# ELU parts of a feed-forward layer: the result of the max stays in its PSUM bank

## The chip, the cores and the metric

The kernel runs on one core of one Trainium2 chip. The metric is the device time of one execution in microseconds (us). The core has five engines that work at the same time: TensorE (PE, matrix products, with its weight load PEld), VectorE (DVE), ScalarE (ACT), GpSimd (POOL) and SyncE (SP, which issues most transfers). TensorE writes its products into PSUM, a small memory of eight banks; one bank holds 128 x 512 float32. VectorE and ScalarE read and write PSUM and the large on-chip memory SBUF.

## The reference

Three layers in a row on 2304 tokens (4 batches of 576) of width 512:

```python
x = attention(q, k, v)            # landmark attention, 8 heads of 64
h = x @ w_in                      # 512 -> 2048
g = np.where(h > 0, h, np.exp(np.minimum(h, 0)) - 1)     # ELU
x = g @ w_out                     # 2048 -> 512
out = mixture_of_experts(x)       # top 2 of 8 experts, 512 -> 1024 -> 512
```

The change lies in the second layer, between the two products.

## The kernel before

The feed-forward layer works on six chunks of tokens (512, 256 and four times 384 columns) and on 16 blocks of 128 hidden features. A *part* c.f is block f of chunk c; there are 96 parts. Each value is carried as a float16 high half and a float16 low half, and each product is three float16 products.

The order of all work ahead of the experts is written out by hand: `ORDER` is a list of tokens, and each engine runs its own instructions in the order of that list. Work of the attention (tokens such as `2:nm.1`), the conversion of weights (`I`, `Wa`, `Wb`), the routing (`RA` to `RS`) and the feed-forward layer are mixed in it. One part goes through these tokens:

- `L1.c.f` (line 678): 6 to 12 matmuls put h into a PSUM tile `h`, one bank. The tag "l1" has two banks.
- `X` (ACT): e = exp(h) into an SBUF tile `e`. The tag "el" has two buffers.
- `T` (ACT or DVE line 702, as the last letter says): e becomes min(e, 1) - 1 (or its negative), in place.
- `S` (DVE line 706): e = max(e * scale, h), in place in SBUF. This is the last reader of the bank.
- `H` (ACT): the high half g[:, 0] = float16(e).
- `O` (DVE or POOL line 711): the low half g[:, 1] = e - g[:, 0]. This is the last reader of `e`. [...]
- `L2.c.f.t` (line 718): three matmuls for each 128 tokens add the part's share to the output tile `y`.

All elementwise ACT work is recorded at line 215. A new product `h` gets, of the two banks of its tag, the one whose last use stands earliest in the recorded program, also where that use is recorded after the product's own token. So the banks don't strictly alternate: the tokens `S` are not always in the order of the tokens `L1`. TensorE runs its list in order: while a product waits for its bank, everything behind it on TensorE waits too.

Of the kernel before, what the change touches and what calls it, by code (L numbers as in the profile page):

```python
# [13 lines left out]
ALU = mybir.AluOpType  # L14
# [36 lines left out]
ORDER = """  # L51
# [128 lines left out]
def attn_ffn_moe_kernel(ctx: ExitStack, tc: tile.TileContext, q: bass.AP, k: bass.AP, v: bass.AP,  # L180
# [18 lines left out]
    V, A, G, T = nc.vector, nc.scalar, nc.gpsimd, nc.tensor  # L199
# [14 lines left out]
    def act(o, i, f=AF.Copy, **kw):  # L214
        return A.activation(o, i, f, **kw)  # L215
# [451 lines left out]
            lo += n  # L667

    HX = {}

    def l1(c, f):
        p = ps.tile([128, 512], F32, tag="l1", bufs=2, name=f"h{c}_{f}")[:, :CHUNKS[c][1]]
        fs = slice(128 * (f % 8), 128 * (f % 8) + 128)
        for b, o, n, c0 in segments(c):
            i = 0
            for g in range(2):
                for x, y in ((0, 0), (0, 1), (1, 0)):
                    T.matmul(p[:, c0:c0 + n], GT[b, f // 8][:, g, x, fs], AT[b][:, g, y, o:o + n],  # L678
                             start=(i == 0), stop=(i == 5))
                    i += 1  # L680
        HX[c, f] = [p]

# [11 lines left out]
    def elu(c, f, part, e=V):  # L694
        x = HX[c, f]
        if part == "X":
            x.append(sf.tile([128, 512], F32, tag="el", bufs=2, name=f"e{c}_{f}")[:, :CHUNKS[c][1]])
            act(x[1], x[0], AF.Exp, scale=1.0 / S_H)
        if part == "T":
            x.append(S_H if e is V else -S_H)  # L700
            if e is V:
                V.tensor_scalar(x[1], x[1], 1.0, 1.0, op0=ALU.min, op1=ALU.subtract)
            else:
                act(x[1], x[1], AF.Relu, scale=-1.0, bias=1.0)
        if part == "S":
            V.scalar_tensor_tensor(x[1], x[1], x[2], x[0], op0=ALU.mult, op1=ALU.max)  # L706
        if part == "H":
            HT[c, f] = sf.tile([128, 2, 512], F16, tag="gT", bufs=3, name=f"g{c}_{f}")[:, :, :CHUNKS[c][1]]
            act(HT[c, f][:, 0], x[1])
        if part == "O":  # L710
            e.tensor_tensor(out=HT[c, f][:, 1], in0=x[1], in1=HT[c, f][:, 0], op=ALU.subtract)  # L711
# [555 lines left out]
    for n in "XTSHO":  # L1267
        CMD[n] = lambda c, f, *e, n=n: elu(c, f, n, *e)
# [23 lines left out]
    for e in range(1, NE):  # L1292
# [12 lines left out]
        for i, f0 in enumerate((0, 2)):  # L1305
            more[f0, 1] = [(ew_split, e, j, k) for j in ((6 + i,) if e > 1 else (4 + i, 6 + i)) for k in range(2)]
            x, y = (3, 4) if last else (4, 3)
# [29 lines left out]
    with tc.If(peak > CAP):  # L1337
# [5 lines left out]
        with tc.For_i(0, NE, 1) as e:  # L1343
            V.tensor_scalar(ef, ef, 1.0, None, op0=ALU.add)
            nb = nc.values_load(blocks[0:1, bass.ds(e, 1)], min_val=0, max_val=(NT - CAP + 127) // 128)
            with tc.If(nb > 0):
# [4 lines left out]
                for src, dst, kn, nm, scale in ((w1, w1x, 1, "a", S_W1), (w2, w2x, 2, "b", S_W2)):  # L1351
                    for j in range(4):
# [6 lines left out]
                                               op1=ALU.subtract)  # L1359
                with tc.For_i(0, nb, 1) as i:  # L1360
# [7 lines left out]
                                           op1=ALU.mult)  # L1368
# [56 lines left out]
```

## Time and profile before

| | us |
|---|---|
| median of 3 runs | 784.09 |
| the three runs | 787.2, 784.09, 781.5 |
| the profiled execution | 778.33 |
| its span, first to last instruction | 776.6 |
| PE busy in the span | 752.7 (97%) |
| DVE busy | 619.1 (80%) |
| ACT busy | 427.5 (55%) |
| POOL busy | 279.4 (36%) |

The feed-forward layer lies between 54.6 and 395 us. The profile lists busy time per engine, the waits of each engine with what ended them, and a timeline of instructions. Ends of matmuls are modelled, so a short wait of PE can hide behind the modelled end of the matmul before it.

### The profile page before, as it was taken

How to read it: one execution, taken by the hardware profiler on the slowest of the kernel's cores; microseconds unless marked ns; L12 is line 12 of the kernel's file. 1: busy time of each engine (PE TensorE's matmuls, PEld its weight loads, DVE VectorE, ACT ScalarE, POOL GpSimd, SP SyncE). 2: the span in 40 equal slices, each digit the busy share in tenths (PEclk: the TensorE clock that was granted, in tenths of full speed). 3: DMA queues.
4: the chain of work that ended last, by engine and by line, in shares of the span. 5: the costliest groups of instructions: out<-in, count | busy, mean ns of one | idle time of the engine just before them, and what ended most of it. 6: DMA issues, size and time to landing. Idle time of an engine off the chain costs nothing.

```text
span 776.6 us, 17554 instructions
## 1 busy us (share of the span) xinstructions
PE 752.7 (97%) x6978; PEld 442.5 (57%) x6979; DVE 619.1 (80%) x1352; ACT 427.5 (55%) x820; POOL 279.4 (36%) x302
## 2 busy tenths in 40 slices
PE   8879999999999999999999999999999999999997
PEld 6444444555445446655454874756747576574754
DVE  4999998877886776837547689989999999999851
ACT  2778778646466455546433364656555455664520
POOL 1576566454351222231404252424343332302322
PEclk9999999999999999999999999999999999999999
DMA  9998676786395715523435876673848657382481
GB/s 347 280 299 210 171 243 167 213 180 190 98 255 89 168 42 146 152 87 80 124 42 145 143 248 99 155 186 49 253 73 230 116 135 203 44 241 28 79 268 67
DMA packets 136200, 123.19 MB, mean 159 GB/s; under 512 B 102891, under 2 KB 105963, under 8 KB 136016
## 3 DMA queue, kind: packets, MB, share of 16 engines
q1 hardware_dynamic: 125392, 100.67, 47.9%
q0 software_dynamic: 10720, 21.34, 12.7%
q8 instruction: 56, 0.92, 0.5%
q14 instruction: 32, 0.26, 0.1%
HBM read 70.62 MB, written 39.76 MB: 142 GB/s over the span
## 4 chain that ended last, share of the span: by engine, by line
PE 91%; DVE 5%; DMA 1%; ACT 1%; issue 1%; SPq 0%; POOL 0%; POOLq 0%; DVEq 0%; ACTq 0%
PE y L718 24%; PE ey L1161 21%; PE eb L1066 19%; PE h L678 12%; PE eh L1124 3%; PE ey L1167 3%; PE pg L645 2%; PE ey L1164 2%; DMA q<-in_q_dram 1%; PE pu L483 1%; PE pcv L548 1%; PE l1b L339 1%; PE pe L535 1%; DVE ax L596 0%; DVE woc L259 0%
## 5 line engine op out<-in xcount | busy, mean ns | idle before, releaser
L718 PE MATMUL y<-wout,g 128*128 128x512 f16 x864 | 205.8, 380 | 0.8 <-issue 0.6
L1161 PE MATMUL ey<-w,eh 128*128 128x512 f16 x768 | 167.4, 379 | 0.0
L1187 POOL DMA_INDIRECT acc<-eo,tk x35 | 73.5, 2101 | 204.5 <-ACT eo L215 88.7
L718 PEld LDWEIGHTS <-g 128*128 128x128 f16 x864 | 80.6, 98 | 93.8 <-issue 9.3
L1161 PEld LDWEIGHTS <-eh 128*128 128x128 f16 x768 | 75.0, 98 | 89.0
L678 PE MATMUL h<-AT,G 128*128 128x192 f16 (+3 forms) x768 | 108.0, 286 | 1.4 <-DVE e L706 1.2
L711 POOL TENSOR_TENSOR g<-e,g 128x384 f16<-128x384 f32 (+2 forms) x44 | 43.8, 996 | 135.8 <-ACT g L215 121.1
L678 PEld LDWEIGHTS <-G 128*128 128x128 f16 x768 | 63.7, 98 | 43.6 <-issue 6.2
L215 ACT ACTIVATE eh<-c 128x300 f16<-128x300 f32 x112 | 47.7, 453 | 63.0 <-DVE c L1083 59.0
L215 ACT ACTIVATE g<-e 128x384 f16<-128x384 f32 (+2 forms) x96 | 49.4, 519 | 48.0 <-PE y L718 28.6
L215 ACT ACTIVATE eo<-ey,ws 128x512 f32<-128x512 f32 (+3 forms) x60 | 32.4, 541 | 68.7 <-PE ey L1161 40.2
L215 ACT ACTIVATE e<-h 128x384 f32<-128x384 f32 (+2 forms) x96 | 46.4, 487 | 38.9 <-PE h L678 24.4
L706 DVE SCALAR_TENSOR_TENSOR e<-e,h 128x384 f32<-128x384 f32 (+2 forms) x96 | 52.3, 549 | 15.2 <-ACT e L215 12.6
L903 POOL DMA_INDIRECT xs<-rows,pos x36 | 37.0, 1027 | 58.1 <-DVE mcum L887 26.9
L942 DVE SCALAR_TENSOR_TENSOR w<-ew,w 128x1024 f16<-128x1024 f32 x36 | 44.6, 1261 | 13.2 <-ACT w L215 13.2
L1066 PE MATMUL eb<-tx,wpC 128*128 128x300 f16 x336 | 47.4, 291 | 0.0
L1095 DVE SCALAR_TENSOR_TENSOR eh<-c,eh 128x300 f16<-128x300 f32 x112 | 46.1, 463 | 1.0
L711 DVE TENSOR_TENSOR g<-e,g 128x384 f16<-128x384 f32 (+2 forms) x52 | 29.5, 572 | 13.6 <-ACT g L215 10.8
L1066 PEld LDWEIGHTS <-wpD 128*128 128x128 f16 x336 | 32.7, 97 | 11.0 <-issue 0.9
L1066 PEld LDWEIGHTS <-wpB 128*128 128x128 f16 x336 | 32.8, 98 | 10.0
L1066 PEld LDWEIGHTS <-wpC 128*128 128x128 f16 x336 | 32.7, 97 | 10.2
L1083 DVE TENSOR_TENSOR c<-eb,u 128x300 f32<-128x300 f32 x84 | 36.6, 461 | 1.7 <-PE eb L1066 1.5
(263 smaller groups left out, 1359.9 us busy)
## 6 DMA issues: line engine op xcount, KB each, us to landing
ew<-in_moe_w_dram SPq DMA_DIRECT2D x64, 512.0 KB
wi<-in_moe_w_in_dram SPq DMA_DIRECT2D x16, 512.0 KB
wo<-in_moe_w_out_dram SPq DMA_DIRECT2D x16, 512.0 KB
q<-in_q_dram SPq DMA_DIRECT2D x8, 576.0 KB
k<-in_k_dram SPq DMA_DIRECT2D x8, 576.0 KB
v<-in_v_dram SPq DMA_DIRECT2D x4, 1152.0 KB
out_dram<-acc SPq DMA_DIRECT2D x1, 4608.0 KB
xs<-zrow SPq DMA_DIRECT2D x3, 1300.0 KB
```

Source lines behind the costliest of these rows:

```text
L215: return A.activation(o, i, f, **kw)
L678: T.matmul(p[:, c0:c0 + n], GT[b, f // 8][:, g, x, fs], AT[b][:, g, y, o:o + n], start=(i == 0), stop=(i == 5))
L706: V.scalar_tensor_tensor(x[1], x[1], x[2], x[0], op0=ALU.mult, op1=ALU.max)
L711: e.tensor_tensor(out=HT[c, f][:, 1], in0=x[1], in1=HT[c, f][:, 0], op=ALU.subtract)
L718: T.matmul(YP[c, t], h[:, x, 128 * t:128 * t + 128], WOUT[f][:, y], start=(f == 0 and i == 0), stop=(f == 15 and i == 2))
L903: n = nc.gpsimd.indirect_dma_start(out=xs[:, :], out_offset=bass.IndirectOffsetOnAxis(ap=R["pos"][:, i // 2, i % 2:i % 2 + 1], axis=0), in ...
L942: V.scalar_tensor_tensor(dst[1][:, ks, :], t, scale, dst[0][:, ks, :], op0=ALU.mult, op1=ALU.subtract)
L1066: T.matmul(p, w_op(e, w, s, k, f), x_op(e, x, t, k), start=(i == 0 and k == 0), stop=(i == 2 and k == 1))
L1083: V.tensor_tensor(out=o, in0=EB[n, f], in1=EU[a, f], op=ALU.add)
L1095: V.scalar_tensor_tensor(lo, o, 0.0, hi, op0=ALU.max, op1=ALU.subtract)
L1161: T.matmul(p, EH[e, f][:, x, 128 * j:128 * j + 128], W2T[e][y][:, f, :], start=start, stop=stop)
L1187: nc.gpsimd.indirect_dma_start(out=acc[:, :], out_offset=bass.IndirectOffsetOnAxis(ap=TK[e][:live(j), j:j + 1], axis=0), in_=EO[e, j], in_ ...
```

## The change

For parts whose `O` runs on VectorE and stands in `ORDER` ahead of the second next token `L1`, `S` writes its result into the PSUM bank that holds h instead of into `e`. `H` and `O` then read the bank. 20 of the 96 parts meet the test: 0.1, 1.2, 1.14, 2.4, 2.10, 2.14, 2.15, 3.1, 3.7, 3.8, 3.10, 3.13, 4.0, 4.5, 4.11, 5.2, 5.7, 5.8, 5.14 and 5.15. For these the tile `e` is last used by `S`, and the bank is last used by `O`.

```diff
     HX = {}
+    at = {x: i for i, x in enumerate(ORDER.split())}
+    hs = [x for x in at if x[:3] == "L1."]
+    direct = set()
+    for i, x in enumerate(hs):
+
+        o = at.get(f"O{x[2:]}.V")
+        if o and (i + 2 >= len(hs) or o < at[hs[i + 2]]):
+            direct.add(x[3:])
...
         if part == "S":
-            V.scalar_tensor_tensor(x[1], x[1], x[2], x[0], op0=ALU.mult, op1=ALU.max)
+            o = x[0] if f"{c}.{f}" in direct else x[1]
+            V.scalar_tensor_tensor(o, x[1], x[2], x[0], op0=ALU.mult, op1=ALU.max)
+            x[1] = o
```

No instruction is added, removed or moved on any engine. What moves is which tiles the 60 instructions `S`, `H` and `O` name, which bank 32 of the products get, and who waits for whom. The products behind a changed part in the bank that the built program gives it: h0_2 behind part 0.1, h1_5 behind 1.2, h3_11 behind 3.10, h4_2 behind 4.0. Two products get the other bank than before, since a changed part now keeps its own bank longer: h2_11, which stood behind part 2.10, now stands behind 2.12 (whose `S` is on VectorE just ahead of the `O` of 2.10), and h3_10, which stood behind 3.8, now stands behind 3.9 (whose `S` is recorded after h3_10).

VectorE around part 0.1, the kernel before (`S` is L706, `O` is L711; the name ahead of the arrow is written, those behind it are read, and the brackets name the engines waited for):

```order
L706 SCALAR_TENSOR_TENSOR e0_1_772<-e0_1_772,h0_1_750 128x512 [waits Activation_49]
L292 SCALAR_TENSOR_TENSOR wout0_634<-wo2_389,wout0_634 128x512
L711 TENSOR_TENSOR g0_0_782<-e0_0_769,g0_0_782 128x512 [waits Activation_49]
L259 TENSOR_SCALAR win2_257<-wi21_522 128x512
L260 SCALAR_TENSOR_TENSOR wi21_522<-wi21_522,win2_257 128x512
L711 TENSOR_TENSOR g0_1_797<-e0_1_772,g0_1_797 128x512 [waits Activation_49]
```

The same place with the change (`S` is L715, `O` is L721):

```order
L715 SCALAR_TENSOR_TENSOR h0_1_750<-e0_1_772,h0_1_750 128x512 [waits PE_49,Activation_49]
L292 SCALAR_TENSOR_TENSOR wout0_634<-wo2_389,wout0_634 128x512
L721 TENSOR_TENSOR g0_0_782<-e0_0_769,g0_0_782 128x512 [waits Activation_49]
L259 TENSOR_SCALAR win2_257<-wi21_522 128x512
L260 SCALAR_TENSOR_TENSOR wi21_522<-wi21_522,win2_257 128x512
L721 TENSOR_TENSOR g0_1_797<-h0_1_750,g0_1_797 128x512 [waits Activation_49]
```

The bank of h0_1 is now last read by the last of these rows, before by the first. The next product in that bank, h0_2, waits for VectorE in both kernels: before until the first row is done, now until the last.

TensorE at the product h2_11, the kernel before:

```order
L718 MATMUL y21_2629<-wout2_1147,g2_9_2989 128x512
L483 MATMUL pu23_3090<-R23_3045 32x64 [waits DVE_49]
L483 MATMUL pu23_3090<-R23_3045 32x64 x7
L678 LDWEIGHTS G11_1857
L678 MATMUL h2_11_3101<-AT1_1708,G11_1857 128x384
```

With the change:

```order
L728 MATMUL y21_2629<-wout2_1147,g2_9_2989 128x512
L483 MATMUL pu23_3090<-R23_3045 32x64 [waits DVE_49]
L483 MATMUL pu23_3090<-R23_3045 32x64 x7
L686 LDWEIGHTS G11_1857
L686 MATMUL h2_11_3101<-AT1_1708,G11_1857 128x384 [waits DVE_49]
```

Before, the first matmul of h2_11 had no wait of its own; now it waits for VectorE, for the `S` of part 2.12.

## Rows read from the trace of the kernel before

**Rows 1.** The page: span, then busy us, share of the span, instructions of each engine.
```profile
span 776.6 us, 17554 instructions
PE 752.7 (97%) x6978; PEld 442.5 (57%) x6979; DVE 619.1 (80%) x1352; ACT 427.5 (55%) x820; POOL 279.4 (36%) x302
```

**Rows 2.** Windows, the feed-forward stretch: length, then busy PE, PEld, DVE, ACT, POOL, clock.
```profile
54.60:395.00 340.40, 333.68 (x3133) 173.44 (x3132) 258.19 (x662) 209.76 (x446) 133.61 (x166) 1.00 0.59 152
```

**Rows 3.** The page's chain of work that ended last, by engine.
```profile
PE 91%; DVE 5%; DMA 1%; ACT 1%; issue 1%; SPq 0%; POOL 0%; POOLq 0%; DVEq 0%; ACTq 0%
```

**Rows 4.** Waits of PE in that stretch: us in total, times, longest.
```profile
PE pu L483 <- issue: 2.1, 3, 1.3
PE pa L431 <- ACT lT L215: 1.8, 1, 1.8
PE h L678 <- DVE e L706: 1.2, 2, 1.0
```

**Rows 5.** Timeline of PE: where h0_2, h1_5, h2_11, h3_10, h3_11, h4_2 start.
```profile
60.22 1.02 PE L678 MATMUL h<-AT,G 128*128 128x512 f16 x4
...
138.46 0.83 PE L678 MATMUL h<-AT,G 128*128 128x64 f16 x12
...
211.41 1.15 PE L678 MATMUL h<-AT,G 128*128 128x384 f16 x6
...
268.03 1.14 PE L678 MATMUL h<-AT,G 128*128 128x384 f16 x6
...
275.42 1.14 PE L678 MATMUL h<-AT,G 128*128 128x384 f16 x6
...
298.70 1.07 PE L678 MATMUL h<-AT,G 128*128 128x192 f16 x11
```

**Rows 6.** Timeline of DVE: S and O of 0.1; O 1.2; S 2.12, O 2.10; S 3.9; O 3.10; O 4.0.
```profile
59.49 0.68 DVE L706 SCALAR_TENSOR_TENSOR e<-e,h 128x512 f32<-128x512 f32 x1
...
62.48 0.68 DVE L711 TENSOR_TENSOR g<-e,g 128x512 f16<-128x512 f32 x1
...
138.87 0.43 DVE L711 TENSOR_TENSOR g<-e,g 128x256 f16<-128x256 f32 x1
...
212.59 0.55 DVE L706 SCALAR_TENSOR_TENSOR e<-e,h 128x384 f32<-128x384 f32 x1 [0.75 <-ACT e L215]
213.06 0.55 DVE L711 TENSOR_TENSOR g<-e,g 128x384 f16<-128x384 f32 x1
...
269.04 0.52 DVE L706 SCALAR_TENSOR_TENSOR e<-e,h 128x384 f32<-128x384 f32 x1
...
275.19 0.54 DVE L711 TENSOR_TENSOR g<-e,g 128x384 f16<-128x384 f32 x1
...
299.52 0.55 DVE L711 TENSOR_TENSOR g<-e,g 128x384 f16<-128x384 f32 x1
```

**Rows 7.** Groups by form: busy us and mean ns of one, idle before; DVE, then ACT.
```profile
L653 DVE SCALAR_TENSOR_TENSOR G<-pg,G 128x512 f16<-128x512 f32 x32 | 21.1, 682 | 2.5 <-ACT G L215 2.5
L711 DVE TENSOR_TENSOR g<-e,g 128x512 f16<-128x512 f32 x6 | 4.1, 679 | 0.0
...
L215 ACT ACTIVATE g<-e 128x384 f16<-128x384 f32 x64 | 33.0, 520 | 38.2 <-PE y L718 25.7 <-DVE e L706 9.6 <-DVE gw L846 0.8
L215 ACT ACTIVATE e<-h 128x384 f32<-128x384 f32 x64 | 31.1, 487 | 30.6 <-PE h L678 18.1 <-DVE g L711 6.7 <-PE pq L483 2.1
```

**Rows 8.** Waits of ACT in the feed-forward stretch: us in total, times, longest.
```profile
ACT g L215 <- PE y L718: 28.6, 23, 5.2
ACT e L215 <- PE h L678: 24.4, 29, 2.1
...
ACT e L215 <- DVE g L711: 7.3, 12, 1.1
```

**Rows 9.** Windows, columns as in rows 2: the one fall of the clock, and before it.
```profile
30.85:34.26 3.41, 1.81 (x37) 0.80 (x22) 3.37 (x10) 2.48 (x8) 2.44 (x3) 1.00 0.91 255
34.26:37.67 3.41, 3.41 (x27) 1.66 (x24) 3.23 (x8) 2.02 (x5) 2.93 (x3) 0.52 1.08 225
```

## The prediction, on record before the changed kernel ran

> **What bounds the kernel now.** I read the page first: PE is busy for 752.7 us of a span of 776.6 [rows 1], and the chain of work that ended last runs through PE for 91% [rows 3]. So TensorE is the bound, and a change pays or costs by what it does to PE's idle time. The change lies between 54.6 and 395 us, so I read that stretch alone next: PE busy 333.68 of 340.40 us at full clock, DVE 258.19, ACT 209.76 [rows 2]. PE's idle time there is 340.40 - 333.68 = 6.72 us, and its longest items are not this change's business: 2.1 us of issue and 1.8 us for a tile of the attention. Only 1.2 us is a product h that waits for `S` to free a bank [rows 4]. Then the timeline: for each of the 20 changed parts I looked for the product that gets the same bank next, took its start on PE, and compared it with the end of `O`, which is to free the bank from now on.
>
> **The scale.** The profiled execution took 778.33 us, 1.7 us more than its span; the median of the runs is 784.09, 5.8 us more. I make the sum on the profiled execution and carry the difference over to the median. What a measurement of this kernel can tell from no change is about 1%, 7.8 us.
>
> **The change part by part.** No instruction comes or goes on any engine, and no transfer. There are four edits in effect.
>
> *The bank is held longer, through `H` and `O`.* This is the cost. Where PE gets to the next product only after the end of `O`, it is free. In 16 of the 20 parts that is so, to within a few hundredths of a us. In four it is not:
>
> - h0_2 started at 60.22, at the end of `S` (59.49 + 0.68 = 60.17). `O` ended at 62.48 + 0.68 = 63.16 [rows 5, 6]. VectorE runs four other instructions between the two, back to back, and has no reason to do otherwise. PE waits 63.16 - 60.17 = 2.99 us more.
> - h1_5 started at 138.46; `O` of 1.2 ended at 138.87 + 0.43 = 139.30 [rows 5, 6]. With 0.04 us from the end to the start (60.22 - 60.17 = 0.05 is the pattern), 0.88 us.
> - h3_11 started at 275.42; `O` of 3.10 ended at 275.19 + 0.54 = 275.73 [rows 5, 6]: 0.35 us.
> - h4_2 started at 298.70; `O` of 4.0 ended at 299.52 + 0.55 = 300.07 [rows 5, 6]: 1.41 us. Its token is recorded ahead of that `O`, so the edit's test didn't see it.
>
> *Two products change banks.* A changed part keeps its bank until `O`, so the pool gives its follower the other bank.
>
> - h2_11 now stands behind 2.12. It started at 211.41; `S` of 2.12 ended at 212.59 + 0.55 = 213.14 [rows 5, 6]: 1.77 us. Had it stayed behind 2.10, the wait would be until 213.06 + 0.55 = 213.61, 2.2 us.
> - h3_10 now stands behind 3.9. It started at 268.03; `S` of 3.9 ended at 269.04 + 0.52 = 269.56 [rows 5, 6]: 1.57 us.
>
> The other 30 products that change banks would find them free at the times of this trace.
>
> Sum of the six: 2.99 + 0.88 + 0.35 + 1.41 + 1.77 + 1.57 = 8.97 us. All are waits on TensorE, whose list runs in order, so what stands behind is late by as much: `L2` matmuls, the attention's small products, and with them ACT and DVE. Do the waits add, or does each swallow the next? They add if VectorE's `S` and `O` move along with PE. Mostly they do: ACT waited 24.4 us in 29 places for a product h and 28.6 us in 23 places for y [rows 8], and DVE's `S` at 212.59 itself waited for ACT [rows 6]. PE's present waits can give a little back where their releaser doesn't move; for that I take off 0.5 us, an eighth of the 2.1 + 1.8 us of the two longest [rows 4], an estimate.
>
> *`e` comes free earlier, at `S` in place of `O`.* Two parts later, `X` can start earlier. ACT waited 7.3 us in 12 places for a DVE `O` to free `e` [rows 8]. That is ACT's idle time, and ACT is busy for 209.76 of 340.40 us [rows 2]. It is worth something only where PE waits for what follows; the row for that is PE's 1.2 us [rows 4]. I take 0, with a gain of 1.2 us as the other end.
>
> *The operands lie in PSUM.* `H` reads a bank: the ACT rows that do so take 487 ns against 520 for the present `H` [rows 7], 33 ns x 20 = 0.7 us on an engine with room: 0. `O` reads one input from a bank: the DVE row with that kind of operands, L653, takes 682 ns against 679 for `O` with both in SBUF, at 512 columns [rows 7]: 0. `S` now writes the bank that it reads. No row shows VectorE writing to PSUM. The low end is its present price, 0.55 us; for the high end I let it double, +0.55 us, as if reads and writes of one bank took turns. On six waits that makes at most 6 x 0.55 = 3.3 us more. The rows nearest to it (PSUM as a source) show no price, so I take 0 and keep 3.3 us for the range.
>
> [...]
>
> **Forecast:** 8.97 - 0.5 = 8.5 us longer: 786.8 us on the scale of the profiled execution, 792.6 on that of the median, 1.1% slower. That is just past the bound of 1%, so the word "slower" is hardly likelier than "same", though a gain is unlikely.
>
> **The rivals.**
>
> *Half is given back.* PE's own waits shrink when it arrives later: those of 2.1 and 1.8 us [rows 4], if code and ACT are ready at the old times. For it: both releasers (issue, ACT) aren't the products that are delayed. Against it: ACT's tile depends on earlier PE work. Then 8.97 - 3.9 = 5.1 us: 789.2, within 1%.
>
> *Only the first wait counts.* After it PE is 2.99 us later. If VectorE does not move along, the other five (each at most 1.77 us) are gone, since all their releasers would be early enough. For it: VectorE still has 82 us free in this stretch [rows 2]. Against it: rows 8, above. Then 3.0 us: 787.1, within 1%.
>
> *Not slower: the freed `e` wins.* The point from which it decides: `X` two parts on starts earlier by up to 7.3 us in all [rows 8], so `S`, `H` and `O` follow earlier, and at the six places the bank is free before PE gets there. At 60.22 this can't be, as VectorE is busy through. At the others, margins of 0.35 to 1.77 us stand against waits of at most 1.1 us [rows 5, 6, 8]. If all went, PE's 1.2 us went too, against the 2.99 us that stays if VectorE doesn't; at best -1.2 us: 782.9. More than 1% faster is out of reach: it needs 7.8 us, and PE's whole idle time in the stretch is 6.72 us [rows 2].
>
> [...]
>
> **How the numbers follow.** Chances: forecast 0.55, with the clock's fall or a dearer `S` inside it up to 796.5 (0.15 of the 0.55); half given back 0.22; first wait only 0.13; no wait or a gain 0.10. Predicted is the likeliest, 792.5. The range reaches down over both middle rivals, 787.1 less the some 2 us by which medians of such runs may lie apart (the three runs spread over 5.7 us), to 785; and up to 797 for the dear `S` or the clock. Of the forecast's 0.55, some 0.46 lie over 784.09 x 1.01 = 791.9, and 0.02 of the others: slower 0.48. Faster by over 1% could come from the measurement alone: 0.03. Within 1%: 0.49.
>
> **What would show it.** In the profile of the changed kernel PE should have new waits in front of h, released by DVE: one near 60 us of some 2.9 us released by the `O` line, others at h1_5, h2_11, h3_10 and h4_2 of 0.8 to 1.8 us; PE's waits for h should rise from 1.2 us to 8 or 10. PE's busy time should stay. ACT's waits for `O` should fall below 7.3 us, its `g<-h` take 0.49 us, `O` 0.55 us, and `S` into the bank 0.55 us, or up to 1.1 if reads and writes of a bank take turns. The prediction is wrong if the stretch from the first h to the last y is not 6 us longer; if the waits are there and the end is not late, then PE had slack behind it that I didn't see. If the waits are missing, VectorE ran ahead.

## The result and the profile after

The changed kernel takes 792.32 us in the median of 12 runs (788.75 to 794.86), the kernel before 784.14 on the same chip (780.66 to 787.51): ratio 1.0105, 95% interval 1.0085 to 1.0125. That is slower by 1.1%, 8.2 us. Measured again among the experiments it was 1.0142 [1.0116, 1.0167] and 1.0143 [1.0120, 1.0166], some 11 us, each beside other runs of the kernel before. Two executions far off all others, of 888 us (e3_hold) and 2735 us (the kernel before beside it), are left out of the ratios. The profiled execution took 788.75 us, the shortest of its twelve, 10.4 more than that of before.

In the changed kernel h is line 686, `S` 715, `O` 721, y 728. The page first: span, the busy engines, and the chain that ended last, by engine [rows 1, 3].

```profile
span 787.1 us, 17548 instructions
PE 754.8 (96%) x6978; PEld 444.2 (56%) x6979; DVE 618.9 (79%) x1352; ACT 427.4 (54%) x820; POOL 281.5 (36%) x302
...
PE 81%; DVE 7%; issue 4%; DMA 3%; POOL 2%; ACT 1%; SPq 0%; POOLq 0%; DVEq 0%; ACTq 0%
```

PE counts as busy for 2.1 us more, with the same number of matmuls, some of them at a clock of 0.51 (below), and the span is 10.5 us longer: the rest is idle time of PE. In the chain PE has gone from 91% to 81%, DVE from 5% to 7%, issue from 1% to 4%: the chain now leaves PE more often for what PE waits for. Next the feed-forward stretch, with the columns of rows 2.

```profile
54.60:404.00 349.40, 335.25 (x3134) 174.25 (x3133) 257.96 (x661) 210.43 (x447) 132.91 (x167) 1.00 0.58 149
```

The stretch is 9.0 us longer [rows 2], PE's idle time in it 349.40 - 335.25 = 14.15 us in place of 6.72. The waits of PE there name the cause [rows 4]: h waits 8.9 us, where it waited 1.2.

```profile
PE h L686 <- DVE g L721: 5.1, 4, 3.0
PE h L686 <- DVE e L715: 3.8, 4, 1.8
PE pu L483 <- issue: 2.2, 2, 1.1
PE pa L431 <- ACT lT L215: 2.0, 1, 2.0
```

Now the six places of the prediction, on PE's timeline: h0_2, h1_5, h2_11, h3_10, h3_11, h4_2. A row gives start, length and, in brackets, the idle time ahead of it with its releaser [rows 5].

```profile
63.73 1.46 PE L686 MATMUL h<-AT,G 128*128 128x512 f16 x6 [2.98 <-DVE g L721]
...
142.84 0.83 PE L686 MATMUL h<-AT,G 128*128 128x64 f16 x12 [0.69 <-DVE g L721]
...
216.28 1.14 PE L686 MATMUL h<-AT,G 128*128 128x384 f16 x6 [1.76 <-DVE e L715]
...
274.28 2.08 PE L686 MATMUL h<-AT,G 128*128 128x384 f16 x6 [0.84 <-DVE e L715]
...
283.46 1.14 PE L686 MATMUL h<-AT,G 128*128 128x384 f16 x6 [0.20 <-DVE g L721]
...
308.16 1.15 PE L686 MATMUL h<-AT,G 128*128 128x192 f16 x12 [1.25 <-DVE g L721]
```

All six wait, and the brackets name the lines that were forecast: `O` (721) at four, `S` of another part (715) at h2_11 and h3_10. DVE's timeline shows what ended them: `S` and `O` of 0.1, `O` of 1.2, `S` of 2.12, `S` of 3.9, `O` of 3.10, `O` of 4.0 [rows 6].

```profile
60.02 0.68 DVE L715 SCALAR_TENSOR_TENSOR h<-e,h 128x512 f32<-128x512 f32 x1
...
63.00 0.68 DVE L721 TENSOR_TENSOR g<-h,g 128x512 f16<-128x512 f32 x1
...
142.36 0.42 DVE L721 TENSOR_TENSOR g<-h,g 128x256 f16<-128x256 f32 x1
...
215.67 0.56 DVE L715 SCALAR_TENSOR_TENSOR e<-e,h 128x384 f32<-128x384 f32 x1 [0.73 <-ACT e L215]
...
273.71 0.51 DVE L715 SCALAR_TENSOR_TENSOR e<-e,h 128x384 f32<-128x384 f32 x1
...
282.87 0.54 DVE L721 TENSOR_TENSOR g<-h,g 128x384 f16<-128x384 f32 x1
...
307.56 0.55 DVE L721 TENSOR_TENSOR g<-h,g 128x384 f16<-128x384 f32 x1
```

At the first place `O` ends at 63.00 + 0.68 = 63.68 and h0_2 starts at 63.73. The prices of the new operands, as groups by form (busy us, mean ns of one), DVE and then ACT [rows 7]:

```profile
L715 DVE SCALAR_TENSOR_TENSOR e<-e,h 128x384 f32<-128x384 f32 x47 | 25.7, 550 | 7.0 <-ACT e L215 5.6 <-issue 0.3
L721 DVE TENSOR_TENSOR g<-e,g 128x384 f16<-128x384 f32 x21 | 11.7, 560 | 5.0 <-issue 2.7 <-ACT g L215 2.2
L715 DVE SCALAR_TENSOR_TENSOR h<-e,h 128x384 f32<-128x384 f32 x17 | 9.5, 556 | 6.0 <-ACT e L215 5.7
L721 DVE TENSOR_TENSOR g<-h,g 128x384 f16<-128x384 f32 x17 | 9.4, 553 | 7.2 <-ACT g L215 7.2
...
L215 ACT ACTIVATE g<-h 128x384 f16<-128x384 f32 x17 | 8.3, 488 | 8.4 <-DVE h L715 3.9 <-PE y L728 3.8 <-DVE gw L888 0.7
```

`S` into the bank that it reads takes 556 ns against 550 into SBUF, `O` out of the bank 553 against 560, `H` 488 ns. So the operands cost nothing, and `H` is some 30 ns shorter than out of SBUF (520 ns in [rows 7]). ACT's waits [rows 8]:

```profile
ACT e L215 <- PE h L686: 33.2, 36, 2.2
ACT g L215 <- PE y L728: 30.4, 27, 3.7
...
ACT e L215 <- DVE g L721: 3.1, 7, 1.0
```

The freed `e` does what it says: ACT waits 3.1 us for `O` in place of 7.3. But ACT waits 8.8 us more for h, because h is late.

At last the clock [rows 9]. The window ahead of the one fall in this stretch, and the fall; the profile of before has none in the stretch:

```profile
270.34:273.75 3.41, 1.30 (x9) 0.56 (x9) 0.94 (x4) 0.68 (x2) 0.97 (x2) 1.00 0.42 160
273.75:277.17 3.42, 2.89 (x9) 1.31 (x9) 2.55 (x6) 0.98 (x2) 0.00 (x0) 0.51 0.42 150
```

PE was busy for 1.30 of 3.41 us, and then had a clock of 0.51 for 3.42 us: (1 - 0.51) x 3.42 = 1.7 us, if PE would have worked all through it.

### The profile page after: what moved, and what is told of

It reads as the page before. It is cut to its first block, busy times and chain, and to the rows that moved or that the text cites. A ratio compares the mean times of both kernels' runs of the same rounds, so it can differ in the third digit from the quotient of the medians.

```text
span 787.1 us, 17548 instructions
## 1 busy us (share of the span) xinstructions
PE 754.8 (96%) x6978; PEld 444.2 (56%) x6979; DVE 618.9 (79%) x1352; ACT 427.4 (54%) x820; POOL 281.5 (36%) x302
## 4 chain that ended last, share of the span: by engine, by line
PE 81%; DVE 7%; issue 4%; DMA 3%; POOL 2%; ACT 1%; SPq 0%; POOLq 0%; DVEq 0%; ACTq 0%
PE y L728 22%; PE ey L1171 18%; PE eb L1076 17%; PE h L686 11%; PE eh L1134 3%; PE ey L1177 2%; PE pg L645 2%; DMA v<-in_v_dram 2%; PE ey L1174 1%; DMA q<-in_q_dram 1%; POOL out_dram L1214 1%; POOL xs L913 1%; DVE x L391 1%; POOL base L1224 1%; PE pu L483 1%
## 5 line engine op out<-in xcount | busy, mean ns | idle before, releaser
L1197 POOL DMA_INDIRECT acc<-eo,tk x35 | 75.9, 2167 | 202.9 <-ACT eo L215 77.3
L721 POOL TENSOR_TENSOR g<-e,g 128x384 f16<-128x384 f32 (+2 forms) x44 | 43.6, 990 | 143.5 <-ACT g L215 126.0
L215 ACT ACTIVATE e<-h 128x384 f32<-128x384 f32 (+2 forms) x96 | 46.6, 487 | 43.1 <-PE h L686 33.2
L215 ACT ACTIVATE g<-e 128x384 f16<-128x384 f32 (+2 forms) x76 | 39.3, 521 | 38.1 <-PE y L728 26.0
L952 DVE SCALAR_TENSOR_TENSOR w<-ew,w 128x1024 f16<-128x1024 f32 x36 | 44.5, 1260 | 12.3 <-ACT w L215 10.5
L715 DVE SCALAR_TENSOR_TENSOR e<-e,h 128x384 f32<-128x384 f32 (+2 forms) x76 | 41.7, 550 | 11.3 <-ACT e L215 9.2
L215 ACT ACTIVATE w<-ew 128x1024 f16<-128x1024 f32 x36 | 37.0, 1050 | 0.2
```

The source lines that it names most:

```text
L715: V.scalar_tensor_tensor(o, x[1], x[2], x[0], op0=ALU.mult, op1=ALU.max)
L952: V.scalar_tensor_tensor(dst[1][:, ks, :], t, scale, dst[0][:, ks, :], op0=ALU.mult, op1=ALU.subtract)
L1197: nc.gpsimd.indirect_dma_start(out=acc[:, :], out_offset=bass.IndirectOffsetOnAxis(ap=TK[e][:live(j), j:j + 1], axis=0), in_=EO[e, j], in_ ...
```

## Experiments

Each was measured beside the kernel before on the same chip, in four groups with medians of before of 779.79, 776.08, 780.24 and 776.08 us. In the table, "us over" is the ratio's part over 1 times that median, "new waits" what PE's waits for h, released by `S`, `O` or a reading of the bank, come to in the profile of the stretch, less the 1.2 us of before (in e12_fill 3.0 us of discarded work on PE come on top of the 4.8), and the clock is the mean granted clock of the runs compared, of the kernel and of before.

| run | ratio, 95% interval | us over | new waits for h | clock, before's |
|---|---|---|---|---|
| e1_six | 1.0161 [1.0126, 1.0196] | 12.6 | 8.9 | 0.9885, 0.9941 |
| e2_fourteen | 1.0007 [0.9986, 1.0028] | 0.5 | 0.0 | 0.9938, 0.9941 |
| e3_hold | 1.0166 [1.0132, 1.0199] | 12.9 | 9.3 | 0.9914, 0.9941 |
| e4_first | 1.0036 [1.0015, 1.0058] | 2.8 | 3.0 | 0.9939, 0.9941 |
| e5_after | 1.0142 [1.0116, 1.0167] | 11.0 | 7.5 | 0.9907, 0.9941 |
| e6_five | 1.0059 [1.0036, 1.0083] | 4.6 | 4.6 | 0.9958, 0.9941 |
| e7_early | 1.0093 [1.0068, 1.0118] | 7.2 | 6.6 | 0.9937, 0.9941 |
| e8_moved | 1.0038 [1.0017, 1.0059] | 2.9 | 1.6 | 0.9946, 0.9941 |
| e9_order | 1.0021 [1.0001, 1.0041] | 1.6 | 0.0 | 0.9934, 0.9944 |
| e10_after | 1.0143 [1.0120, 1.0166] | 11.1 | 6.8 | 0.9910, 0.9945 |
| e11_six | 1.0142 [1.0121, 1.0164] | 11.0 | 7.5 | 0.9914, 0.9945 |
| e12_fill | 1.0080 [1.0063, 1.0098] | 6.2 | 4.8 | 0.9962, 0.9945 |

### Which of the twenty parts cost (e1_six, e2_fourteen, e4_first, e6_five)

```diff
-            direct.add(x[3:])
...
+    direct = set("0.1 1.2 2.10 3.8 3.10 4.0".split())       # e1_six; e4_first: "0.1" alone;
+                                                            # e6_five: these without "0.1"
+    direct = set("1.14 2.4 2.14 2.15 3.1 3.7 3.13 4.5 4.11 5.2 5.7 5.8 5.14 5.15".split())  # e2_fourteen
```

> Only the parts 0.1, 1.2, 2.10, 3.8, 3.10 and 4.0 write S into the bank: those whose longer hold makes one of the six waits by the trace of before. Theory (PE waits for its bank at six products): the whole loss stays, +8 to +9 us against the kernel before, ratio 1.010 to 1.012, with PE's waits for h at the same six products. Rival (each S, H or O on PSUM operands costs something of its own): 6 of 20 of the loss, +2.5 us, ratio 1.003.

> Only the other fourteen parts write S into the bank. Theory: no product waits longer, so 0 us, ratio 0.999 to 1.001; PE's waits for h stay near 1.2 us. Rival (price of the operands): 14 of 20 of the loss, +5.7 us, ratio 1.007. Third (the tile e that comes free earlier is a gain which the six waits hide): a gain of up to 1.2 us, ratio 0.9985.

> Only part 0.1 writes S into the bank. Theory (the waits add): +3.0 us, ratio 1.0038, one wait of 2.9 to 3.0 us at h0_2. Rival (only the first wait counts, the later ones are gone because VectorE did not move along): nearly the whole measured loss, +8 us. Rival (PE has slack behind it): 0 us with the wait there.

> Only the parts 1.2, 2.10, 3.8, 3.10 and 4.0 stay in their banks; the first one, 0.1, goes through SBUF as before. Theory (the waits add): 0.88 + 1.77 + 1.57 + 0.35 + 1.41 = 6.0 us of waits, no stop near 60 us; ratio 1.006 to 1.010 with the falls of the clock. With the first alone (3.3 us) it makes up the six. Rival (only the first wait counts, the later ones are swallowed by a late TensorE): here the first is missing, so the first of the five, 0.9 us, counts and the rest is swallowed: 1 to 2 us, ratio 1.001 to 1.003.

The fourteen parts behind which nothing waits cost 0.5 us, with an interval that includes zero, and gain nothing either; the six make the whole loss, with 12.6 us even more than the 8 to 9 expected. The first alone costs 2.8 us and the other five 4.6 us: that the first wait swallows the rest is refuted. PE's waits for h of e4_first, and of e6_five, in which h is line 679, `S` 708 and `O` 714:

```profile
PE h L679 <- DVE g L714: 3.0, 1, 3.0
PE h L679 <- DVE e L708: 1.2, 2, 1.0
```

```profile
PE h L679 <- DVE e L708: 3.6, 4, 1.6
PE h L679 <- DVE g L714: 2.2, 3, 1.2
```

In both, the time over before is close to what the waits are longer (2.8 against 3.0 us, 4.6 against 4.6); of the five, 6.0 us of waits were expected, and h3_10 waits only 0.8 of its 1.57 there. The two don't make up the six: 2.8 + 4.6 = 7.4 us. The six in e1_six are not so simple: 12.6 us against 8.9 us of waits, at a clock lower by 0.0056. That became the second question.

### The bank or the operands (e3_hold)

The kernel before, with its results in SBUF, and behind each of the 20 `O` (`held` lists the parts) one more instruction on VectorE, which reads one column of the bank:

```diff
         if part == "O":
             e.tensor_tensor(out=HT[c, f][:, 1], in0=x[1], in1=HT[c, f][:, 0], op=ALU.subtract)
+            if f"{c}.{f}" in held:
+                V.tensor_copy(last, x[0][:, 0:1])
```

> The kernel before, with one VectorE instruction more behind the O of each of the 20 parts: it reads one column of the bank of h, so that the bank is held as long as in the change, while S, H and O work in SBUF as before. Theory: the same six waits, each longer by the small instruction (about 0.1 us), +8.5 to +9.5 us, ratio 1.011 to 1.012. Rival (price of the operands): no loss but the 20 small instructions on an engine that is not the bound, 0 to +1 us.

```profile
PE h L680 <- DVE last L715: 5.4, 4, 3.0
PE h L680 <- DVE e L708: 5.1, 4, 2.2
```

Without any operand moved, holding the bank alone makes the loss of the change: 12.9 us, 9.3 us of it waits. The copies take 150 ns each, 3.0 us on VectorE, of which the waits show 0.3. The loss is larger than the 8.5 to 9.5 us expected: beside the waits, the mean clock is lower by 0.0027, which makes 2.1 us of 780, and some 1.5 us stay open. It is the time for which the bank is held, not where `S`, `H` and `O` read or write.

### Shorter waits (e7_early, e8_moved, e9_order) beside the changed kernel (e5_after)

Two edits of `ORDER`: e7_early lets VectorE make `O` of 0.1 ahead of two conversions; e8_moved puts five of the waiting products one to three places later on PE (the first two shown).

```diff
-... H.0.1 nz.0.3 I.10.1 I.9.3 I.11.2 0:ghi.1.1 O.0.1.V ...
+... H.0.1 nz.0.3 O.0.1.V I.10.1 I.9.3 I.11.2 0:ghi.1.1 ...      # e7_early
...
-1:xtr.0.0 L1.0.2 L2.0.0.3 X.0.3 X.0.2 L2.0.0.1 ...
+1:xtr.0.0 L2.0.0.3 X.0.3 L2.0.0.1 L1.0.2 X.0.2 ...              # e8_moved
-... L1.1.5 L2.1.0.0 1:ghi.2.1 S.1.4 L2.1.0.1 H.1.4 ...
+... L2.1.0.0 1:ghi.2.1 S.1.4 L2.1.0.1 L1.1.5 H.1.4 ...
```

> The changed kernel once more, as the measure for the three kernels that run beside it on the same chip. Theory (six waits of about 9.0 us, and on top of them falls of TensorE's clock of about 1.7 us each behind the places where it now stops): 9 to 13 us over the kernel before, ratio 1.011 to 1.016, with a mean clock lower than the kernel before by 0.003 to 0.006. Rival (the other 14 parts give some 3 us back, which is why the six alone came out at 1.016 and all twenty at 1.0105): 8 us, ratio 1.0105, whatever the chip and the clock.

> All twenty parts as in the change, but VectorE makes O of 0.1 ahead of two conversions (I.10.1 and I.11.2), each about 0.6 us, that stand between S and O. Theory (TensorE waits for the end of O, and what it waits is what the end is late): the wait ahead of h0_2 falls from 3.0 to about 1.8 us, and the end comes 1.2 us earlier than in the changed kernel, more if a fall of the clock behind that stop goes too. Rival (the time lies in something else near 60 us, such as the clock or the bank itself): the wait falls and the end does not move.

> All twenty parts as in the change, but five products h (h0_2, h1_5, h2_11, h3_10, h4_2) are issued by TensorE one to three places later in its list, behind other products that are ready, so that less of the bank's wait is left. Theory (the loss is TensorE standing in line at a bank, not the bank's longer use as such): the waits for h fall from 9 us to 4 to 6 us, and the time with them, 3 to 5 us less than the changed kernel. Rival (what stands ahead is only put off: ACT and VectorE get their h later, and TensorE waits for y in place of h): waits for h fall, new waits ahead of y or of the attention's products take their place, and the time stays within 1.5 us of the changed kernel.

The changed kernel is at 786.36 us here, e7_early at 783.06, e8_moved at 778.84, before at 776.08. PE's row in e7_early at h0_2, and PE's waits in e8_moved:

```profile
63.87 1.46 PE L686 MATMUL h<-AT,G 128*128 128x512 f16 x6 [2.05 <-DVE g L721]
```

```profile
PE h L679 <- DVE e L708: 2.1, 3, 1.0
...
PE y L721 <- DVE g L714: 0.8, 1, 0.8
PE h L679 <- DVE g L714: 0.7, 2, 0.5
```

The wait is 0.9 us shorter, 1.2 were expected; the end comes 3.3 us earlier, more than the wait gives; as each of the two intervals is some 2 us to either side, how much more stays open. With the products later, 7.5 us of the changed kernel's 10.3 are gone (786.36 - 778.84), at 2.8 us of waits for h and 0.8 for y; 3 to 5 were expected. All twenty parts still stay in their banks there. The wait for y is the one that the rival names, but it comes with the order and not with the banks: the next run, without any part in its bank, has it too (0.9 us). So what costs is PE standing at the head of its list, not the longer use of a bank.

> The kernel before, all parts through SBUF, with TensorE's list as in the run with five later products h (h0_2, h1_5, h2_11, h3_10, h4_2 issued one to three places later). It is the control of that run, which came out at ratio 1.0038 with 2.8 us of waits for h. Theory (the later places take away the waits and do nothing else): the kernel before has at most 1.2 us of waits for h to lose and gets none of its own from the later places: ratio 0.998 to 1.002, so that the parts in the bank still cost 1 to 4 us in that order. Rival (the later order is itself faster, and hides a loss of 7 us or more that the bank still makes): 775 us or less where the kernel before takes 780, ratio 0.995 or less.

The order alone is no faster than before: 1.0021, at the edge of what was expected, with a wait of 0.9 us for y at the place where e8_moved has its 0.8. The parts in the bank thus cost 1.0038 / 1.0021, 0.2%, in that order, which the two intervals (0.2% to either side each) don't tell from zero, where they cost 1.1 to 1.4% in the old one. No version beat the kernel before.

### The clock (e10_after, e11_six, e12_fill)

e12_fill is the changed kernel with work for PE's longest stop:

```diff
     def l1(c, f):
+        if (c, f) == (0, 2):
+            YP[c, 3] = ps.tile([128, 512], F32, tag="n", bufs=1, name=f"y{c}3")
+            for _ in range(13):
+                T.matmul(YP[c, 3], hot, hot[:, None, :].to_broadcast([128, 4, 128]), start=True, stop=True)
```

> The changed kernel, as the measure for the two that run beside it. 9 to 11 us over the kernel before on any chip, mean clock 0.990 to 0.993 against 0.995.

> The six parts alone a second time, now beside the changed kernel on the same chip. On another chip they came out at ratio 1.0161, with a wait of 2.2 us ahead of h3_10 where the changed kernel has 0.8, and a mean clock of 0.988. Theory (the other 14 parts do nothing; the difference between 1.0161 and the changed kernel is the clock of that chip and one wait that falls in two ways): within 2.5 us of the changed kernel here. Rival (the other 14 give some 3 us back when the six are there): 3 us or more over the changed kernel, outside the interval.

> The changed kernel with 13 products that are thrown away (128x512 each, into the bank of y0_3, which is begun anew by the next product) put into TensorE's list right ahead of h0_2, so that it works through the 3.0 us for which it otherwise stands. Everything waits as long as before; only TensorE's idle time there goes. Theory (on top of the waits the clock falls behind the stop at 60 us, 1.7 us each time, in some of the executions): no wait ahead of h0_2, no fall of the clock near 64 us, and 0.5 to 2 us less than the changed kernel. Rival (the clock has no part in it): the same time as the changed kernel, or up to 0.3 us more for the work thrown away; falls of the clock as often as without.

e11_six is level with the changed kernel (786.13 and 786.50 us), so the fourteen give nothing back that these intervals (1.7 us to either side each) could show; that e1_six was dearer in the first group goes with the lower clock of its runs there and a wait at h3_10 of 2.2 us in place of 0.8 (a pause of TensorE ahead of it, told in the section on why the prediction was right, is missing in e11_six). The filled kernel took 781.78 us, 4.7 less than the changed one, although every bank comes free as late. The same two windows at the stop, of e11_six and then of e12_fill, with the columns of rows 2 (the last but two is the clock):

```profile
60.05:63.46 3.41, 0.74 (x4) 0.22 (x3) 3.41 (x7) 2.38 (x6) 1.19 (x2) 1.00 0.95 344
63.46:66.87 3.41, 3.10 (x8) 1.16 (x8) 2.92 (x3) 1.77 (x3) 3.41 (x3) 0.51 0.91 157
```

```profile
60.05:63.46 3.41, 3.33 (x16) 1.38 (x15) 3.41 (x7) 3.06 (x6) 1.19 (x2) 1.00 0.72 200
63.46:66.87 3.41, 3.32 (x16) 1.54 (x16) 2.44 (x4) 2.30 (x6) 3.41 (x3) 1.00 0.81 135
```

PE busy for 0.74 us, and then half speed; PE busy for 3.33 us, and no fall. And on PE's timeline of e12_fill the stop is the discarded work:

```profile
60.41 2.97 PE L683 MATMUL y<-hot 128*128 128x512 f16 x13
63.55 1.46 PE L690 MATMUL h<-AT,G 128*128 128x512 f16 x6 [0.18 <-DVE g L725]
```

A gain of 0.5 to 2 us was expected: the fall behind the stop is gone, as the theory said, but the size was too small. The mean clock rose from 0.9910 to 0.9962, worth 0.0052 x 785 = 4.1 us, about two falls. That the filling gave all of it isn't shown. The mean takes in the falls ahead of 54 us, of which the profiles of e10_after and e11_six have two and that of e12_fill one. On the timelines e11_six is 0.22 us behind e12_fill at h0_2 and 1.78 us at 113 us, so the filled stop gave 1.56 us; a later 1.9 us come where e11_six has a wait of `pu` of 1.65 us, at 207.6 us, that e12_fill lacks. In the 14 profiles (before, after, and these twelve) the clock fell 10 times between 60 us and the tail in the seven in which PE stood idle at 60 us for the whole 3 us, and once in the seven others. e10_after's own fall came behind another thin place, at 207.5, with PE busy for 2.22 us of the 3.41 ahead of it:

```profile
204.12:207.53 3.41, 2.22 (x122) 1.84 (x121) 2.05 (x16) 0.82 (x3) 0.91 (x1) 1.00 0.23 85
207.53:210.94 3.41, 3.03 (x15) 1.36 (x16) 2.54 (x4) 0.00 (x0) 0.00 (x0) 0.54 0.02 5
```

What the clock of 0.51 costs, the trace shows for the time in which PE works: in the profile after, PE falls 1.43 us further behind the kernel before from h3_10 to the next h (6.25 us late at 274.28, 7.68 at 278.92), and half of the 2.89 us busy in that window is 1.4 us. The rest of the 3.42 us, 0.53, falls into the wait ahead of h3_10 and costs nothing.

## Why the prediction was right

The forecast was 792.5 us, 8.5 us longer; 792.32 and 8.2 were measured. Its mechanism is shown (e3_hold, e8_moved), and its working holds place by place. How far each product starts later than in [rows 5], less the lateness of what runs ahead of it:

| place | predicted us | measured us | from |
|---|---|---|---|
| h0_2 | 2.99 | 2.97 | 63.73 - 60.22 - 0.54 of lateness ahead of the stretch |
| h1_5 | 0.88 | 0.87 | 142.84 - 138.46 - 3.51 |
| h2_11 | 1.77 | 1.83 | 216.28 - 211.41 - 3.04 (the product h ahead: 211.53 - 208.49) |
| h3_10 | 1.57 | 1.66 | 274.28 - 268.03 - 4.59 (`pu` ahead: 269.17 - 264.58) |
| h3_11 | 0.35 | 0.36 | 283.46 - 275.42 - 7.68 (the product h ahead: 278.92 - 271.24) |
| h4_2 | 1.41 | 1.42 | 308.16 - 298.70 less 283.46 - 275.42 |
| sum | 8.97 | 9.11 | |

The rows on which h3_10 and h3_11 rest, before and then after: `pu` and the product h behind h3_10 on PE, and on DVE the instruction that reads `pu`.

```profile
264.58 0.70 PE L483 MATMUL pu<-R 32*32 32x64 f32 x10
271.24 1.15 PE L678 MATMUL h<-AT,G 128*128 128x384 f16 x6
268.13 0.22 DVE L571 TENSOR_TENSOR R<-pu,R 128x64 f32<-128x64 f32 x1 [2.98 <-PE pu L483]
```

```profile
269.17 0.74 PE L483 MATMUL pu<-R 32*32 32x64 f32 x10
278.92 1.15 PE L686 MATMUL h<-AT,G 128*128 128x384 f16 x6
272.81 0.22 DVE L571 TENSOR_TENSOR R<-pu,R 128x64 f32<-128x64 f32 x1 [3.06 <-PE pu L483]
```

- **The sum.** By the starts every term holds to 0.1 us. The bracket at h3_10 shows only 0.84, which misleads: PE pauses at `pu`, a small product of the attention, just ahead of it, 3.55 us from the first matmul of `pu` to its reader before (268.13 - 264.58) and 3.64 after (272.81 - 269.17), so about as long. `S` of 3.9 follows that reader by 0.9 us both times. But before, 0.83 us of the pause are booked as `pu`'s wait for issue (and 0.58 at the y behind it), and after 2.23; in e1_six and e3_hold it is 0.83 and 0.86 again, and the bracket at h3_10 2.2. As ends of matmuls are modelled, the starts are the safer measure of the two. In e5_after to e8_moved and e10_after to e12_fill `pu` doesn't pause there, and h3_10, where it waits, waits 0.8.
- **The waits add.** Right for the waits: 3.0 us (first) and 4.6 us (five) make 7.6, against 7.5 in e11_six, and no wait swallowed another. The rival "only the first counts" is refuted by e6_five. The times do more than add: 2.8 + 4.6 = 7.4 us against 11.0 in e11_six, where the mean clock is lower. VectorE moved along with PE: `S` of 2.12 ran 3.08 us later (215.67 - 212.59), the product h ahead of h2_11 3.04, and ACT waited for h for 33.2 us in place of 24.4.
- **What is given back, 0.5 us.** Not shown. PE's wait for `pa`, which was to shrink, grew from 1.8 to 2.0 us. `pu`'s longest issue wait of before, 1.3 us at 203 us [rows 4], is missing after, and PE is 1.51 us less late behind it. But e2_fourteen, e4_first and e12_fill lack it too, and the nine other runs have it, with the change and without, so I can't lay it to the change.
- **`e` freed earlier, 0.** Right, and it happened: ACT's wait fell from 7.3 to 3.1 us. PE's one wait for ACT in the stretch, for `pa`, is no shorter, and the fourteen parts alone, which free `e` earlier too, gain nothing (e2_fourteen).
- **Operands in PSUM, 0.** Right: 556 ns for `S` into the bank against 550 into SBUF, and 553 against 560 for `O`. The high end, 3.3 us, is refuted.
- **The clock, mis-sized.** The sum has no part for it; the chances have its fall, together with a dearer `S`, at 0.15 and up to 796.5, 4.0 us over the likeliest, and no run shows what the fall adds to that bound. What the runs showed in its place: in the profile after one fall, of which 1.4 us show in PE's starts; over the runs the mean clock is 0.0031 to 0.0056 under that of before for the changed kernel and the six alone, at 785 us that is 2.4 to 4.4 us. So the 11 us of the later groups are some 7 us of waits and some 3 us of clock, with about 1 us left over. In all twelve rows of the table, waits and clock added so come within 1.7 us of "us over", if e12_fill's 3.0 us of discarded work count as a wait. In the first comparison the mean clock of the changed kernel was 0.9896; that of before isn't recorded there, so how its 8.2 us divide stays open. Range and sign held; that the forecast met the median so closely owes something to luck.

The two profiled executions differ by 10.4 us: 0.54 ahead of the stretch, 9.11 at the six places, 1.43 in the stretch at half clock, 0.17 more of wait for `pa`, 1.51 less at the missing wait of `pu`, 0.28 less behind h2_11, which makes h4_2 9.46 us later, and 0.96 behind it, to the end.

Open: why the first stop alone left the mean clock of 12 runs where it was (e4_first, 0.9939), though its profile shows a fall at 64.1 us, while the changed kernel with the same stop filled had a mean clock higher by 0.005. I can't say which stop causes which fall; falls ahead of 54 us came once or twice in every kernel, before included, and they blur the comparison.

## What to carry to other kernels

Leaving a result in its PSUM bank saved nothing here, since TensorE hardly waited for the engines that it relieved (before, 1.8 us for a tile of ScalarE and 1.2 us for `S` of VectorE [rows 4]), and it made the bank's next product wait for the last reader (9.1 us at the six places). With two banks and TensorE as the bound, look up the end of that last reader against the next product's start, in time and not in the order of a list. Check the product that the pool moves to another bank as well: two of the six waits were there. Of the two cures tried for a waiting TensorE, issuing other ready products ahead of the waiting one did more (7.5 us of 10.3) than filling the longest stop with discarded work (4.7 us of 10.4, of which the profiles tie 1.6 to the clock at that stop).

To compare two traces around a pause, take the starts of the same instructions in both: a wait in brackets can shrink because the engine's pause is booked at its neighbour.

## What was not expected of the hardware

Where five more waits followed, a stop of 3.0 us on TensorE went with a loss of more than its 3.0 us (11.0 us with it in e5_after, 4.6 without it in e6_five); alone it cost 2.8 (e4_first). In four of the seven profiles with that stop a fall of the clock, to 0.51 in e11_six, began in the last 1.1 us of it, and lasted 3.4 us, once 6.8 (e4_first). Thirteen products thrown away at that place left the whole kernel 4.7 us faster than the idle engine did. VectorE writing to the very bank that it reads takes 556 ns for 128x384, against 550 into SBUF.
